# When the last three sums of weights are fetched and formed: one by one among the pairs of the first big block, with longer planned transfers

## The chip, the cores and the metric

The kernel runs on one core of a Trainium2 chip. The time is the device time of one execution in microseconds (us). Before the change the median of three runs is 609.46 us (609.19 to 609.64).

## What is computed

Chunked attention with a few memory keys (4 batches, 8 heads, 768 tokens, head width 64), and behind it a feed-forward layer on all 3072 tokens:

```
x = attention(q, k, v, mem_k, mem_v)        # 3072 x 512
h = x @ w_in                                # w_in: 512 x 2048
g = maximum(h, 0) + alpha * minimum(h, 0)
out = g @ w_out                             # w_out: 2048 x 512
```

All is float32. A product of two float32 matrices is made of three matmuls on split values: each operand is held as a high part and a low part, and low x high, high x low and high x high are added up.

## The kernel before

**Blocks.** The tokens are worked on in blocks of 384. Blocks 0 and 1 go through the layer plainly, while the rest of the attention still runs. The other six blocks form three *big blocks* of two blocks each. In a big block, `h = x @ w_in` is made by a scheme with seven products instead of eight for a 2x2 arrangement of halves: the 16 slices of `w_in` are taken in eight pairs, and for pair `i` seven products of 128x384 (named B11, B21, T2, T3, T1, T4, B22) are made by `pair(i)`, each of six matmuls (line 1174), added up on VectorE (`u`, line 1194), bent by alpha (lines 1070 and 1073) and split. Between them `pair(i)` places the second layer's matmuls (`chunk`, line 1109) of the pair before. In the first big block `pair(0)` to `pair(5)` run; the slices of the last two pairs are multiplied plainly ahead of them. Then come the second layer's remaining chunks, with two more rounds of attention between them. The second and third big block run all eight pairs.

**Weights.** A pair needs four quarters of two weight slices (`far_a[i]`, 8 pieces with their sums) and `far_b[i]` (6 pieces). They lie in DRAM and are loaded for each pair (`wa`, 1024 and 768 KB) into slots that two pairs before have given free; the second layer's weights come as `wo` (1024 KB). The original quarters are put out to DRAM while blocks 0 and 1 are worked on (`copy_far`). The *sums of weights*, which the scheme needs beside them, are made by `sum_far(i)`: GpSimd adds and subtracts quarters (`form`, lines 911 and 914), ScalarE rounds the result to the high part (a cast, line 919), GpSimd takes the low part (line 922), and SyncE puts both parts out (`put`, line 925: first to `far_b[i]`, then to `far_a[i]`). For `i` from 0 to 4 the quarters still lie in the core's memory; for the late ones, `i` = 5, 6 and 7 (`FIRST_LATE`), they are fetched back from DRAM first (`fetch`, line 904: `far_r` and the first half of `far_a`, 512 KB each). There is one set of two buffers `form`, so a fetch waits until the put before it has read its buffer out.

**Who needs the late sums.** Pair 5 of the first big block loads what `sum_far(5)` puts out. Sums 6 and 7 are first needed by pairs 6 and 7 of the second big block.

**The order of the work.** `Plan` takes the kernel's steps in program order, each with an engine, a planned cost and what it reads and writes, and sends them out by a list schedule: on each engine the ready step with the longest chain behind it goes first. A planned transfer lands `LAND` = 3.1 us behind its issue, whatever its size. What comes out is one fixed order of instructions for each engine; an engine then works strictly in that order and waits by semaphores. SyncE issues nearly all transfers, also in one order. A key such as `("gate", ...)` exists in the plan alone: it holds a step back in the order, but no semaphore is made from it. In the kernel before, all three late sums are added ahead of the pairs, gated by the last step of the plain blocks.

**Stores.** `leave` copies a finished part of the output to one of five places on its way out; three of these places are the buffers of `sum_far`.

Of the kernel before, what the change touches and what calls it, by code (L numbers as in the profile page):

```python
# [41 lines left out]
NFP = NF // 2  # L42
# [37 lines left out]
ORDER = []  # L80
# [21 lines left out]
COPY_AT = (9, 11, 13, 15, 18, 21, 24, 27)  # L102
SUM_AT = (25, 26, 28, 29, 29)
FIRST_LATE = 5
SPLIT = 0
FIRST_SLOW = 25

# [25 lines left out]
class Plan:  # L133
# [4 lines left out]
    def __init__(self):  # L138
        self.steps, self.wrote, self.read = [], {}, {}

    def add(self, engine, cost, fn, reads=(), writes=(), rest=0.0):
        n = len(self.steps)
        deps = {self.wrote[k] for k in reads if k in self.wrote}
        for k in writes:
            deps |= self.read.pop(k, set())
            if k in self.wrote:
                deps.add(self.wrote[k])
            self.wrote[k] = n
        for k in reads:
            self.read.setdefault(k, set()).add(n)  # L150
        self.steps.append((engine, cost, fn, deps - {n}, rest))

    def send(self):
        users = [[] for _ in self.steps]
        for n, step in enumerate(self.steps):
            for d in step[3]:
                users[d].append(n)
        lag = {PE: HOP, DVE: HOP, ACT: HOP, POOL: HOP, SP: LAND}
        behind = [0.0] * len(self.steps)
        for n in reversed(range(len(self.steps))):  # L160
            engine, cost, _, _, rest = self.steps[n]
            behind[n] = max(rest, cost + max((behind[m] + lag[engine] for m in users[n]), default=0.0))
        for n, more in SHIFT.items():
            behind[n] += more
        left = [len(step[3]) for step in self.steps]
        ready = [0.0] * len(self.steps)
        free = dict.fromkeys(lag, 0.0)
        able = {n for n in range(len(self.steps)) if not left[n]}
        while able:
            at = {}  # L170
            for n in able:
                engine = self.steps[n][0]
                at[engine] = min(at.get(engine, 1e9), max(ready[n], free[engine]))
            engine = min(at, key=at.get)
            n = max((n for n in able if self.steps[n][0] == engine and ready[n] <= at[engine]),
                    key=lambda n: (behind[n], -n))
            able.remove(n)
            _, cost, fn, _, _ = self.steps[n]
            free[engine] = at[engine] + cost
            fn()  # L180
            for m in users[n]:
                wait = lag[engine]
                if self.steps[m][0] == engine:
                    wait = FOLLOW if engine == DVE else 0.0
                ready[m] = max(ready[m], free[engine] + wait)
                left[m] -= 1
                if not left[m]:
                    able.add(m)
# [3 lines left out]
def body(ctx: ExitStack, tc: tile.TileContext, qvw, kw, whole, heads, w_in, w_out, alpha, out):  # L192
# [649 lines left out]

    def leave_at(late):
        n = next(ntmp)
        return MORE[n % len(MORE)] if late else PLACES[n % 2]

    def store(blk, o_ps):
        def copy(tt, at_, o):
            if blk == 1:
                o["t"] = kept[tt]  # L850
                nc.vector.tensor_tensor(out=o["t"], in0=o_ps[tt], in1=o["t"], op=ALU.add)
            else:
                o["t"] = at_[0].tile([P, DM], F32, name="o_t", tag=at_[1])
                nc.scalar.copy(out=o["t"], in_=o_ps[tt])

        def send(tt, o):
            r = blk * BT + tt * P
            nc.sync.dma_start(out=out[r:r + P, :], in_=o["t"])

        for tt in range(NTT):  # L860
            at_ = (None, None, [("tmp", tt)]) if blk == 1 else leave_at(False)
            o = {}
            place = PLACE[blk, NF - 1] + 1
            step(DVE if blk == 1 else ACT, 0.68 if blk == 1 else 0.59, partial(copy, tt, at_, o), reads=okeys(blk),
                 writes=at_[2], rest=rest(place))
            step(SP, 0.75, partial(send, tt, o), reads=at_[2])
# [25 lines left out]
    def sum_far(i, gate):  # L892
# [34 lines left out]
        whole = [[("rs", n, 0), ("rs", n, 1)] + ([("f", n, 1)] if n or late else []) for n in range(2)]  # L927
        if late:
            for n in range(2):
                step(SP, 0.75, partial(fetch, n), reads=gate + [("dr", i) if n else ("da", i, 0)], writes=whole[n] + [("f", n, 0)])  # L930

        def raw_sum(n):
            step(POOL, 1.3, partial(full, n),
# [5 lines left out]
        def form(n, to, key):  # L939
            step(ACT, 0.65, partial(high, n), reads=[("rs", n, 0), ("rs", n, 1)],  # L940
                 writes=[("f", n, 0)] + ([] if n or late else [("f", n, 1)]))
            step(POOL, 1.3, partial(low, n), reads=[("rs", n, 0), ("rs", n, 1), ("f", n, 0)], writes=[("f", n, 1)])
            step(SP, 0.7, partial(put, n, to), reads=[("f", n, 0), ("f", n, 1)], writes=[key])

        a, b = far_a[i], far_b[i]
        raw_sum(0)
# [101 lines left out]
    def big(s):  # L1048
# [7 lines left out]
        def pe(cost, fn, reads, writes):  # L1056
            step(PE, cost, fn, reads=reads, writes=writes, rest=BIG - clock[0])
            clock[0] += cost
# [101 lines left out]
        def pair(i):  # L1160
# [6 lines left out]
            def product(bank, x, weight, name):  # L1167
                xi = FORMS.index(name)

                def go():  # L1170
                    h[bank[1]] = bank_of(bank)
                    for p in range(2):
                        for k, (wk, xk) in enumerate(((0, 1), (1, 0), (0, 0))):
                            nc.tensor.matmul(  # L1174
                                out=h[bank[1]][:, :BT],
                                lhsT=weight(wk, p).bitcast(F32R),
                                rhs=xf[xi][:, xk, p],
                                start=p == 0 and k == 0, stop=p == 1 and k == 2,
                            )

                pe(1.05, go, [("wa", home["i", s, i, x])] + [("X", xi, hl, p) for hl in range(2) for p in range(2)], [bank[2]])

            def copy_out(t, bank):
                def go():
# [57 lines left out]
        def leave(which, tts, end=False):  # L1242
# [11 lines left out]
                (nc.scalar, nc.sync)[i].dma_start(out=out[r:r + P, cols], in_=x["t"][:, cols])  # L1254

            for tt in tts:
                at_, x = leave_at(True), {}
                step(ACT, 0.59, partial(copy, tt, at_, x), reads=[(downs, ups)[which][tt][2]], writes=at_[2],
                     rest=BIG - clock[0])
                if end and tt == NTT - 1:  # L1260
                    for i in range(2):
                        step((ACT, SP)[i], 0.4, partial(send_half, tt, x, i), reads=at_[2])
                else:
                    step(SP, 0.75, partial(send, tt, x), reads=at_[2])
# [26 lines left out]
        if s == 0:  # L1291
# [20 lines left out]
                plain_up(f, 1, n)  # L1312
            for f in range(12, NF):
                load(f)
            for i in range(FIRST_LATE, NFP):
                sum_far(i, [("gate", len(ORDER) - 1)])
        forms(s > 0)
        for i in pairs:
            think()
            if i in AT_PAIR[s]:  # L1320
                meet(AT_PAIR[s][i], ups)
            pair(i)
        last = s == NBIG - 1
        for f in range(2):
            take(f)
            whole(1, f)
# [156 lines left out]
```

## Time and profile before

| | us |
|---|---|
| median of three runs | 609.46 |
| the profiled execution | 609.57 |
| its span (first to last instruction) | 607.8 |
| first product of pair 0 of the first big block | 204.86 |
| last product of pair 5 | 298.00 to 299.04 |
| second layer of the first big block until the next one's first product | to 337.5 |

The profile is of one execution. A page gives busy shares, a granted TensorE clock and the share of the DMA engines; a timeline lists instructions in order, with the idle time ahead of each and, behind an arrow, what ended it. Where an instruction waits for several things, the arrow names the one that came last by the records. "PE" is TensorE, "DVE" VectorE, "ACT" ScalarE, "POOL" GpSimd, and "SPq" the queue of SyncE.

### The profile page before, as it was taken

Reading aid. Unit: us, or ns where it says so; the run is one execution under the profiler, and the core shown is the slowest. Engines: PE = TensorE matmul, PEld = TensorE weight load, DVE = VectorE, ACT = ScalarE, POOL = GpSimd, SP = SyncE. Lnnn points to the kernel's source line nnn. Section 1 sums busy time; section 2 is a strip of 40 time slices with the busy share of each in tenths; the row PEclk is TensorE's granted clock in tenths of the full one; section 3 lists DMA queues with packets and bytes.
Section 4 is the critical chain, followed back from the end, with each engine's and each line's share of the span. In section 5 each row is a group of like instructions: output and inputs, shape, how many; then the busy total and the mean of one; then the engine's idle time right before and its main releaser. Section 6 shows DMA issues by size and latency. Waiting matters only on the chain.

```text
span 607.8 us, 11965 instructions
## 1 busy us (share of the span) xinstructions
PE 578.1 (95%) x4467; PEld 510.5 (84%) x4467; DVE 458.5 (75%) x992; ACT 301.7 (50%) x780; POOL 172.8 (28%) x193
## 2 busy tenths in 40 slices
PE   6999999999999938889999999999999999999997
PEld 4889988988888827779878899999978899999785
DVE  7989999798879918778989968989748476666420
ACT  3888887656666402633655544353544333333421
POOL 5740000058989724441213700000313400000000
PEclk9999999999999977799999999999999999999999
DMA  8999960679866786797898777866796767677821
GB/s 316 392 418 415 412 267 2 221 272 335 279 241 222 254 307 213 268 326 259 320 382 308 260 262 258 297 226 212 284 362 239 248 219 272 210 272 297 312 92 52
DMA packets 43386, 164.12 MB, mean 270 GB/s; under 512 B 4928, under 2 KB 10304, under 8 KB 34624
## 3 DMA queue, kind: packets, MB, share of 16 engines
q1 hardware_dynamic: 43184, 163.23, 73.6%
q8 instruction: 35, 0.57, 0.4%
q14 instruction: 23, 0.19, 0.1%
q10 hardware_dynamic: 144, 0.13, 0.1%
HBM read 132.41 MB, written 30.93 MB: 269 GB/s over the span
## 4 chain that ended last, share of the span: by engine, by line
PE 79%; DMA 12%; DVE 5%; POOL 2%; issue 1%; SPq 0%; ACT 0%; POOLq 0%; DVEq 0%; ACTq 0%
PE b_ps L1109 25%; PE b_ps L1174 23%; PE h_ps L771 11%; PE o_ps L801 11%; DMA wo<-far_o 4%; DMA far_a<-form 3%; PE a_ps L456 2%; DMA form<-far_a 2%; PE s_ps L357 2%; DMA far_b<-form 1%; DVE xf L971 1%; DVE pt L433 1%; POOL form L914 1%; PE a_ps L616 1%; DMA early<-heads 1%; PE o_ps L603 1%
## 5 line engine op out<-in xcount | busy, mean ns | idle before, releaser
L1174 PE MATMUL b_ps<-xf,wa 128*128 128x384 f32 x924 | 179.0, 344 | 17.1 <-ACT u L1186 11.8
L1174 PEld LDWEIGHTS b_ps<-xf,wa 128*128 128x128 f32 x924 | 167.0, 193 | 25.9 <-ACT u L1186 12.3
L1194 DVE TENSOR_TENSOR u<-b_ps,u 128x384 f32<-128x384 f32 x154 | 82.9, 554 | 39.5 <-PE b_ps L1174 35.8
L433 DVE STREAM_TRANSPOSE pt<-e 32x192 f32<-32x192 f32 (+1 forms) x336 | 100.2, 302 | 10.5 <-PE a_ps L456 3.0
L1070 ACT ACTIVATE g<-u 128x384 f32<-128x384 f32 x88 | 45.9, 525 | 96.9 <-DVE u L1194 92.0
L1109 PE MATMUL b_ps<-wo,xh 128*128 128x512 f32 x276 | 86.5, 395 | 0.0
L1109 PE MATMUL b_ps<-wo,gh 128*128 128x512 f32 x276 | 86.1, 393 | 0.0
L412 POOL TENSOR_TENSOR e<-e,den 128x384 f32<-128x384 f32 x24 | 21.5, 911 | 178.1 <-ACT e L391 74.0
L771 PE MATMUL h_ps<-xh,w 128*128 128x384 f32 x256 | 65.4, 336 | 0.0
L1109 PEld LDWEIGHTS b_ps<-wo,gh 128*128 128x128 f32 x276 | 52.1, 189 | 9.9
L1109 PEld LDWEIGHTS b_ps<-wo,xh 128*128 128x128 f32 x276 | 52.0, 189 | 9.6
L1109 PE MATMUL b_ps<-wo,gl 128*128 128x512 f32 x138 | 54.5, 395 | 2.7 <-DMA wo<-far_o 2.7
L1109 PE MATMUL b_ps<-wo,xl 128*128 128x512 f32 x138 | 54.3, 394 | 0.0
L801 PE MATMUL o_ps<-w,xh 128*128 128x512 f32 x168 | 52.5, 394 | 0.0
L1073 DVE SCALAR_TENSOR_TENSOR g<-g,rise,u 128x384 f32<-128x384 f32 x44 | 30.3, 688 | 26.8 <-ACT g L1070 26.3
L771 PEld LDWEIGHTS h_ps<-xh,w 128*128 128x128 f32 x256 | 46.4, 188 | 1.0
L391 ACT ACTIVATE e<-s_ps,mx 128x64 f32<-128x64 f32 x144 | 43.1, 331 | 5.2 <-DVE mx L383 3.3
L771 PE MATMUL h_ps<-xl,w 128*128 128x384 f32 x128 | 43.8, 342 | 0.0
L985 POOL TENSOR_TENSOR plain<-plain 128x384 f32<-128x384 f32 x24 | 27.5, 1163 | 55.1 <-ACT plain L530 53.2
L801 PEld LDWEIGHTS o_ps<-w,xh 128*128 128x128 f32 x168 | 31.5, 188 | 6.1
L1109 PEld LDWEIGHTS b_ps<-wo,gl 128*128 128x128 f32 x138 | 26.1, 189 | 8.7 <-issue 2.2
L801 PE MATMUL o_ps<-w,xl 128*128 128x512 f32 x84 | 32.9, 392 | 0.0
(119 smaller groups left out, 898.6 us busy)
## 6 DMA issues: line engine op xcount, KB each, us to landing
wo<-far_o SPq DMA_DIRECT2D x46, 1024.0 KB, 7.1
wa<-far_a SPq DMA_DIRECT2D x22, 1024.0 KB, 8.7
wa<-far_b SPq DMA_DIRECT2D x22, 768.0 KB, 4.7
w_t<-w_in SPq DMA_DIRECT2D x16, 512.0 KB, 9.6
w_t<-w_out SPq DMA_DIRECT2D x16, 512.0 KB, 9.2
far_o<-w SPq DMA_DIRECT2D x16, 512.0 KB, 7.9
qk<-kw SPq DMA_DIRECT2D x24, 272.0 KB, 4.7
v_t<-qvw SPq DMA_DIRECT2D x24, 256.0 KB, 7.4
```

The costliest lines, as they stand in the source:

```text
L357: nc.tensor.matmul(out=st["s"][h2][g * CH:(g + 1) * CH, n], lhsT=qs[sets(u)][rows, c * CH:(c + 1) * CH], rhs=kbs[sets(u)][rows, t, STARTS[ ...
L391: nc.scalar.activation(out=st["e"][:, i], in_=st["s"][h2][:, n], func=AF.Exp, scale=SCALE, bias=d["mx"][:, u - us[0], n, h2:h2 + 1], accum ...
L412: nc.gpsimd.tensor_tensor(out=st["e"], in0=st["e"], in1=st["den"].broadcast_to([P, NJ * 2, KW]), op=ALU.mult)
L433: nc.vector.transpose(out=pts[u % NPT][quad * CH:(quad + 1) * CH, j, t0:t0 + n1 - n0].rearrange("p t h q -> p (t h) q"), in_=(st["e"], zer ...
L771: nc.tensor.matmul(out=h["ps"][:, :BT], lhsT=ws[f, 0][:, wk, k * P:(k + 1) * P], rhs=parts(blk, k)[1](xk), start=(k == 0 and n == 0), stop ...
L801: nc.tensor.matmul(out=o_ps[tt], lhsT=h[gk][:, tt * P:(tt + 1) * P], rhs=ws[f, 1][:, wk], start=(f == first_f and i == 0), stop=(f == last ...
L985: step(POOL, 0.95, lambda: nc.gpsimd.tensor_tensor(out=plain_at(to[0]), in0=plain_at(a[0]), in1=plain_at(b[0]), op=ALU.subtract), reads=[a ...
L1070: nc.scalar.activation(out=h[name], in_=src(), func=AF.Relu, scale=-1.0)
L1073: nc.vector.scalar_tensor_tensor(out=to() if to else h[name], in0=h[name], scalar=rise[:, f:f + 1], in1=src(), op0=ALU.mult, op1=ALU.add)
L1109: nc.tensor.matmul(out=o[which][tt], lhsT=h[gk][:, tt * P:(tt + 1) * P], rhs=w[:, wk].bitcast(F32R), start=(f == turns[which][0] and i == ...
L1174: nc.tensor.matmul(out=h[bank[1]][:, :BT], lhsT=weight(wk, p).bitcast(F32R), rhs=xf[xi][:, xk, p], start=p == 0 and k == 0, stop=p == 1 an ...
L1194: nc.vector.tensor_tensor(out=h[t], in0=h[bank[1]][:, :BT], in1=h[t if of is None else of], op=ALU.add)
```

## The change

Sum 5 is now added ahead of pair 1 and gated by pair 0's last product, sum 6 ahead of pair 4 and gated by pair 3, and sum 7 behind the last pair (pair 5) and gated by it. So the late sums begin behind the first, the fourth and the sixth pair. In the plan a late fetch now lands 8.0 us later than before (11.1 us in all), and a late put 4.0 us later. The first big block's `leave` uses three places for its stores instead of five, so that it leaves the two `form` buffers alone.

```diff
+LATE_AT = {1: 5, 4: 6}
+FETCH = 8.0
...
-    def add(self, engine, cost, fn, reads=(), writes=(), rest=0.0):
+    def add(self, engine, cost, fn, reads=(), writes=(), rest=0.0, more=0.0):
...
-                wait = lag[engine]
+                wait = lag[engine] + more
...
     def leave_at(late):
         n = next(ntmp)
-        return MORE[n % len(MORE)] if late else PLACES[n % 2]
+        return MORE[n % (2, 3, len(MORE))[late]]
...
-                step(SP, 0.75, partial(fetch, n), reads=gate + [("dr", i) if n else ("da", i, 0)], writes=whole[n] + [("f", n, 0)])
+                step(SP, 0.75, partial(fetch, n), reads=gate + [("dr", i) if n else ("da", i, 0)], writes=whole[n] + [("f", n, 0)], more=FETCH)
...
-            step(SP, 0.7, partial(put, n, to), reads=[("f", n, 0), ("f", n, 1)], writes=[key])
+            step(SP, 0.7, partial(put, n, to), reads=[("f", n, 0), ("f", n, 1)], writes=[key], more=FETCH / 2 if late else 0.0)
...
-                pe(1.05, go, [("wa", home["i", s, i, x])] + [("X", xi, hl, p) for hl in range(2) for p in range(2)], [bank[2]])
+                pe(1.05, go, [("wa", home["i", s, i, x])] + [("X", xi, hl, p) for hl in range(2) for p in range(2)],
+                   [bank[2]] + ([("pair", i)] if name == "B22" else []))
...
-                at_, x = leave_at(True), {}
+                at_, x = leave_at(1 if s == 0 else 2), {}
...
-            for i in range(FIRST_LATE, NFP):
-                sum_far(i, [("gate", len(ORDER) - 1)])
         forms(s > 0)
         for i in pairs:
+            if s == 0 and i in LATE_AT:
+                sum_far(LATE_AT[i], [("pair", i - 1)] if i else [("gate", len(ORDER) - 1)])
             think()
...
         last = s == NBIG - 1
+        if s == 0:
+            sum_far(NFP - 1, [("pair", pairs[-1])])
```

What becomes of this in the engines' orders is seen at three places. The first is ScalarE in pairs 0 and 1 of the first big block (`u`, `g`, `xh` and `gh` are the pairs' own steps, `form` a late sum's cast). Before:

```order
L1186 COPY u_2898<-b_ps_2870 128x384
L1070 ACTIVATE g_2925<-u_2898 128x384
L1085 CAST xh_209<-g_2925 128x384
L1070 ACTIVATE g_2961<-u_2949 128x384
L919 CAST form_2836<-form_2836 128x512
L1070 ACTIVATE g_2984<-u_2937 128x384
L1070 ACTIVATE g_2990<-u_2911 128x384
L919 CAST form_2900<-form_2900 128x512
L1186 COPY u_3002<-b_ps_2977 128x384
```

And with the change:

```order
L1189 COPY u_2897<-b_ps_2869 128x384
L1072 ACTIVATE g_2920<-u_2897 128x384
L1087 CAST xh_209<-g_2920 128x384
L1072 ACTIVATE g_2954<-u_2942 128x384
L1072 ACTIVATE g_2967<-u_2931 128x384
L1072 ACTIVATE g_2983<-u_2908 128x384
L1189 COPY u_2993<-b_ps_2971 128x384
```

The two casts of sum 5, which stood ahead of pair 1's copy of a product out of its bank, are gone from here. They stand now around pair 3's copy:

```order
L921 CAST form_2969<-form_2969 128x512
L1072 ACTIVATE g_3265<-u_3155 128x384
L1189 COPY u_3269<-b_ps_3246 128x384
L1087 CAST xh_215<-g_3230 128x384
L921 CAST form_2979<-form_2979 128x512
```

The second place is SyncE's queue while pairs 0 to 2 run (`wa<-far_a2` and `far_b2` are pair 2's weights, and so on; `form<-` is a fetch, `<-form` a put). Before:

```order
L904 DMA form_2900<-far_a5_232 128x1024
L295 DMA qk1_190<-qvw 128x384
L1035 DMA wa_2958<-far_b2_237 128x1536
L1035 DMA wa_2972<-far_a2_229 128x2048
L925 DMA far_b5_240<-form_2836 128x1024
L904 DMA form_3017<-far_r6_244 128x1024
L925 DMA far_a5_232<-form_2900 128x1024
L904 DMA form_3029<-far_a6_233 128x1024
L1035 DMA wa_3072<-far_b3_238 128x1536
```

And with the change:

```order
L1037 DMA wa_2951<-far_b2_237 128x1536
L1037 DMA wa_2964<-far_a2_229 128x2048
L906 DMA form_2969<-far_r5_243 128x1024
L906 DMA form_2979<-far_a5_232 128x1024
L1037 DMA wa_3054<-far_b3_238 128x1536
L1037 DMA wo_3073<-far_o3_249 128x2048
L1037 DMA wa_3098<-far_a3_230 128x2048
```

The puts of sum 5 and the fetches of sum 6 have left this stretch: the puts follow behind pair 4's loads, and the fetches of sum 6 stand on either side of pair 5's `wa<-far_a5`.

The third place is SyncE's queue around the end of pair 5 (`wo<-far_o` are the second layer's weights for the chunks that follow). Before:

```order
L1035 DMA wo_3716<-far_o2_248 128x2048
L1035 DMA wo_3733<-far_o3_249 128x2048
L1035 DMA wo_3745<-far_o1_247 128x2048
L1035 DMA wo_3789<-far_o4_250 128x2048
L1250 DMA out<-o_t_3813 128x512
```

And with the change:

```order
L927 DMA far_b6_241<-form_3373 128x1024
L927 DMA far_a6_233<-form_3392 128x1024
L1037 DMA wo_3701<-far_o2_248 128x2048
L906 DMA form_3712<-far_r7_245 128x1024
L906 DMA form_3720<-far_a7_234 128x1024
L1037 DMA wo_3775<-far_o1_247 128x2048
L1037 DMA wo_3782<-far_o3_249 128x2048
```

Sum 6's puts and sum 7's fetches stand ahead of and between the second layer's loads now. Sum 7's two puts stand 15 and 24 places behind its second fetch, among the remaining chunks' loads.

More of the change, by code (lines that the diff above doesn't have):

```diff
@@ L150, in add @@
             self.read.setdefault(k, set()).add(n)
-        self.steps.append((engine, cost, fn, deps - {n}, rest))
+        self.steps.append((engine, cost, fn, deps - {n}, rest, more))
     def send(self):
@@ L160, in send @@
         for n in reversed(range(len(self.steps))):
-            engine, cost, _, _, rest = self.steps[n]
+            engine, cost, _, _, rest, _ = self.steps[n]
             behind[n] = max(rest, cost + max((behind[m] + lag[engine] for m in users[n]), default=0.0))
@@ L177, in send @@
             able.remove(n)
-            _, cost, fn, _, _ = self.steps[n]
+            _, cost, fn, _, _, more = self.steps[n]
             free[engine] = at[engine] + cost
@@ L860, in store @@
         for tt in range(NTT):
-            at_ = (None, None, [("tmp", tt)]) if blk == 1 else leave_at(False)
+            at_ = (None, None, [("tmp", tt)]) if blk == 1 else leave_at(0)
             o = {}
```

## The prediction, made before the changed kernel ran

> **What bounds the kernel now.** I read the windows of busy time first, one for each stage around the change.
>
> ```profile
> core 0: us, PE busy (x) PEld busy (x) DVE busy (x) ACT busy (x) POOL busy (x), PEclk, DMA share, GB/s
> 204.90:217.40 12.50, 12.50 (x66) 11.32 (x66) 9.54 (x21) 3.08 (x7) 5.08 (x5) 1.00 0.69 224
> 217.40:229.20 11.80, 0.02 (x1) 0.00 (x0) 1.55 (x2) 2.47 (x6) 4.49 (x5) 0.64 0.72 274
> 229.20:245.50 16.30, 13.02 (x77) 11.50 (x77) 11.46 (x27) 4.26 (x10) 7.38 (x8) 0.81 0.72 250
> 245.50:271.60 26.10, 24.46 (x111) 22.19 (x111) 20.43 (x45) 11.88 (x41) 12.69 (x12) 0.88 0.79 288
> 271.60:299.00 27.40, 27.40 (x248) 25.32 (x249) 24.32 (x64) 13.07 (x45) 3.96 (x4) 0.94 0.78 276
> 299.00:337.50 38.50, 37.28 (x394) 29.95 (x393) 34.42 (x93) 22.58 (x83) 9.81 (x10) 1.00 0.94 342
> ```
>
> TensorE is the bound everywhere but in one place: from 217.4 to 229.2 us it does nothing, and behind that its granted clock is 0.81 and 0.88. This is the stage of the six pairs. TensorE's timeline gives its edges and waits:
>
> ```profile
> 204.86 11.17 PE L1174 MATMUL b_ps<-xf,wa 128*128 128x384 f32 x60 [0.27 <-DVE plain L1073]
> ...
> 229.24 2.29 PE L1174 MATMUL b_ps<-xf,wa 128*128 128x384 f32 x6 [11.82 <-ACT u L1186]
> ...
> 245.53 4.21 PE L1174 MATMUL b_ps<-xf,wa 128*128 128x384 f32 x12 [3.28 <-ACT plain L530]
> ...
> 271.60 4.96 PE L1174 MATMUL b_ps<-xf,wa 128*128 128x384 f32 x18 [1.60 <-DVE u L1194]
> ...
> 298.00 1.21 PE L1174 MATMUL b_ps<-xf,wa 128*128 128x384 f32 x6
> ```
>
> The three waits inside the stage make 11.82 + 3.28 + 1.60 = 16.7 us. What stands behind them is read from ScalarE's timeline:
>
> ```profile
> 212.21 0.53 ACT L1070 ACTIVATE g<-u 128x384 f32<-128x384 f32 x1 [0.87 <-DVE u L1194]
> 226.57 0.62 ACT L919 CAST form<-form 128x512 fp32r<-128x512 f32 x1 [13.84 <-DMA wa<-far_b]
> ...
> 228.71 0.47 ACT L1186 COPY u<-b_ps 128x384 f32<-128x384 f32 x1
> ...
> 244.07 0.62 ACT L919 CAST form<-form 128x512 fp32r<-128x512 f32 x1 [5.42 <-POOL form L914]
> ...
> 264.83 0.62 ACT L919 CAST form<-form 128x512 fp32r<-128x512 f32 x1 [4.62 <-POOL form L914]
> ```
>
> ScalarE stands for 13.84, 5.42 and 4.62 us ahead of a late sum's cast, and the copy that frees TensorE's bank is queued behind that cast. The arrow of the first wait names a load of `wa`, which a cast of `form` has no need of; I take it for a neighbour in time, since GpSimd and SyncE show the true chain:
>
> ```profile
> 224.48 1.26 POOL L911 TENSOR_TENSOR form<-form 128x512 f32<-128x512 f32 x1 [10.63 <-DMA form<-far_a]
> ...
> 211.38 0.59 SPq L925 DMA_DIRECT2D far_a<-form  x1
> 220.06 0.32 SPq L904 DMA_DIRECT2D form<-far_a  x1
> ```
>
> GpSimd waits 10.63 us for the fetch; that was issued at 220.06 only, 8.7 us behind the put that had to read the same buffer out.
>
> **What the change removes.** By the orders above, pair 1's copy has no cast ahead of it any more. I build the stage again without its waits, from steady rows of the third big block and this stage's attention steps:
>
> ```profile
> 496.43 4.33 PE L1174 MATMUL b_ps<-xf,wa 128*128 128x384 f32 x24
> 500.60 0.39 PE L1109 MATMUL b_ps<-wo,gl 128*128 128x512 f32 x1
> ...
> 501.30 0.39 PE L1109 MATMUL b_ps<-wo,gl 128*128 128x512 f32 x1
> ...
> 512.06 0.39 PE L1109 MATMUL b_ps<-wo,xl 128*128 128x512 f32 x1
> ...
> 284.86 1.20 PE L357 MATMUL s_ps<-qk 64*32 64x64 f32 x96
> 285.99 1.54 PE L456 MATMUL a_ps<-pt,v_t 128*64 128x96 f32 x32
> 287.46 3.41 PE L1174 MATMUL b_ps<-xf,wa 128*128 128x384 f32 x18
> ```
>
> 24 matmuls (four products) take 500.60 - 496.43 = 4.17 us, so a product 1.04; a chunk of three takes 0.70; a whole pair (seven products, six chunks) 512.06 - 500.60 = 11.46. Scores take 1.13 us and attention outputs 1.47. The stage has pair 0 with seven products alone (7.3), five full pairs (57.3), one round of scores and two of outputs (4.1): **68.7 us**. It took 298.00 + 1.04 - 204.86 = 94.2. So **25.5 us** are lost: 16.7 by waits, 0.3 of rounding and gaps, and 8.5 by the clock. The clock's part is seen in the same rows: the six matmuls at 229.24 took 2.29 us where six take 1.04, the twelve at 245.53 took 4.21 where twelve take 2.08; and the windows agree, 16.3 x 0.19 + 26.1 x 0.12 + 27.4 x 0.06 = 7.9 us.
>
> The page "TensorE: Matmul & The Clock Gate" of the Trainium skill (The HAM clock gate) says that the array runs at half clock after an idle window of about 3.4 us and again at full clock after about 3.4 us of work. By that rule only the 11.82 us wait costs clock for certain, 1.7 us, and the whole gain would be some 18.7 us in place of 25.5. The rows disagree: behind waits of 3.28 and 1.60 us the matmuls are slow as well, so the sum goes by the rows.
>
> **What it adds: casts, fetches, puts.** Nothing new is computed; each late sum keeps its two fetches, two casts, GpSimd steps and two puts. The question is whether the moved ones wait again. Sum 5's fetches now follow pair 2's loads, which wait for pair 0's end, 204.86 + 7.3 = 212.2. Queued behind them on SyncE are pair 3's loads, and these wait for pair 1's last uses of their slots, about 10 us later, so no load is held. The casts stand around pair 3's first copy; pair 3 starts at 212.2 + 11.5 + 11.5 + 1.5 = 236.7.
>
> ```profile
> wa<-far_a SPq DMA_DIRECT2D x6, 1024.0 KB, 9.5
> ...
> form<-far_a SPq DMA_DIRECT2D x3, 512.0 KB, 4.3
> ```
>
> A fetch lands 4.3 us behind its issue; even at 9.5, what a load of twice the size took in this stretch, it is there by 224, and four GpSimd steps of 1.3 us at most (the L911 row) end by 230. That leaves 6 us before the cast. Sum 6 is fetched when pair 3 ends, 248.2, and cast in pair 5, which starts at 248.2 + 11.5 + 2.6 = 262.3; sum 7 is cast among the remaining chunks. I cost them at nothing, the pairs' matmuls cover them; if that cover were gone, each would cost what the second and third cast do now (a rival below). Pair 5 needs sum 5's puts: cast at 237 to 239 and with a GpSimd step behind, they go out at about 241, and pair 5's load, which waits for their landing, can go at 248.2 anyway.
>
> **What is late next: VectorE.** From 214.8 us, when it had worked off what was left from the plain blocks, to the stage's end:
>
> ```profile
> 214.80:299.05 84.25, 67.54 (x451) 61.08 (x450) 57.81 (x135) 31.73 (x100) 28.51 (x27) 0.86 0.77 275
> ```
>
> VectorE is busy for 57.81 us there, and TensorE's own need is 68.7 - 9.9 = 58.8: 98%, with both waiting for each other in a fixed order. From 271.6 to 299 VectorE ran at 24.32 / 27.40 = 0.89 with TensorE never idle. At 0.89 the stretch takes 65.0 us (6.2 more than TensorE's need), at 1 it takes nothing more. Since nobody waited for VectorE at 0.89, that row is no ceiling; I take 0.93, nearer to it than to 1: 62.2, so **3.4 us** come back.
>
> **The transfers.** Six of 512 KB (puts and fetches of sums 6 and 7), 3.1 MB, move from the pairs into the stage of remaining chunks, whose engines are 0.94 busy at 342 GB/s; at that rate they are 9.2 us of transfers, against 0.06 x 38.5 = 2.3 us of room: at worst 6.9 us. Not all is due, since loads for the next big block stand at that stage's end. SyncE also waits there: sum 7's fetches wait for sum 6's puts to land, and `wo<-far_o1` is queued behind them.
>
> ```profile
> far_a<-form SPq DMA_DIRECT2D x5, 512.0 KB, 5.0
> ...
> wo<-far_o SPq DMA_DIRECT2D x46, 1024.0 KB, 7.1
> ...
> 308.63 0.47 PE L1109 MATMUL b_ps<-wo,gl 128*128 128x512 f32 x1 [1.22 <-DMA wo<-far_o]
> ```
>
> That stage had one wait for such a load, 1.22 us. The load's slot is free when pair 5 ends; its issue comes about 5 us (a put's landing) behind sum 6's puts, and its first use 12 chunks, 8.3 us, behind the pair, plus 1.1 for the scores that now stand between. Bounds are -1.2 (that wait goes too) and +6.9; I take **+1.0**, nearest to the row. Five places to three for stores and the plan's longer landing only order things: 0, as ScalarE is busy 22.58 of 38.5 us there.
>
> **The sum.** 609.57 (this execution; 0.1 above the median of 609.46) - 25.5 + 3.4 + 1.0 = **588.5 us**, -3.5%. With both ends: 609.6 - 25.5 - 1.2 = 582.9, and 609.6 - 25.5 + 6.2 + 6.9 = 597.2.
>
> **Rivals.**
>
> *VectorE becomes the bound.* If its steps and TensorE's wait for each other as in 245.5 to 271.6 (20.43 of 26.10, 0.78), 57.8 us become 74, so 15 of the 25.5 us come back: 609.6 - 25.5 + 15.3 = 599.4. For it speaks the 98%; against it the 0.89 of a stretch without any wait, and that the 0.78 holds ScalarE's waits that go.
>
> *Transfers bound the remaining chunks.* All 6.9 us at worst, and half clock behind the waits (+2.5 as at 245.53 and after): 609.6 - 25.5 + 3.4 + 9.4 = 596.9. For it speaks 0.94; against it that loads with later dates can give way.
>
> *The casts wait again in their new places*, as the second and third did (3.28 + 1.60, and the clock after them 2.1 + 1.8), some 9 us, with VectorE's 3.4 and 1.0: 597.3. Against it speaks the 6 us of room.
>
> *The change does not take the first wait away*, because the load that the arrow names was the cause: then 11.8 us and 4 of clock stay, 609.6 - 9.7 + 3.4 + 1 = 604.3. Against it: a cast needs no `wa`, and in the new order those loads stand earlier anyway.
>
> *Slower.* SyncE holds the second layer's loads behind sum 6's puts. If these puts wait for GpSimd, and that for attention's steps ahead of it, each us counts from the point where `wo<-far_o1` is issued later than pair 5's end + 9.4 - 7.1 (a load's landing). To eat up 25.5 us the puts would have to be 20 us and more behind pair 5; their casts stand in its first half, so this would need several late landings in a row: over 612.
>
> **Chances.** Forecast (583 to 593) 0.55; VectorE 0.18; transfers 0.10; casts again 0.07; first wait stays 0.04; slower 0.05; nothing either way 0.01. The range of 583 to 599 holds the first, the third, the fourth and half of VectorE's: 0.81. A measurement tells 0.2% from no change here. Faster by more 0.93, within 0.02, slower 0.05.
>
> **What would show it.** Right: pair 1 follows pair 0 without a wait; no cast of `form` has over 2 us of idle time ahead of it in the pairs; granted clock 0.97 and more from 217 to 275; pair 5 ends near 277 instead of 299; VectorE over 0.9 busy. Wrong: a wait of TensorE for `wo` above 3 us behind pair 5, many waits for `u` of VectorE, or SyncE standing at `far_b6`'s put while slots for `wo` are free.

## The result, and the profile after

The changed kernel takes **586.74 us** (median of 4 runs, 585.58 to 587.69) beside 609.33 us (606.64 to 609.64) of the kernel before: ratio **0.9638**, 95% interval 0.9604 to 0.9672. Its profiled execution took 586.14 us with a span of 584.4, so 23.4 us less than the one before in both. One of the four executions of experiment 2 below took 632.85 us at a granted clock of 0.85 and is left out of its ratio. The lines have moved by two or three: L1174, L1109, L919 and L904 of before are L1176, L1111, L921 and L906 now.

The windows of busy time after the change: the six pairs (204.90 to 275.00), the same without what VectorE had left from the plain blocks, the remaining chunks, the second big block's first layer, its first few chunks, and the rest.

```profile
core 0: us, PE busy (x) PEld busy (x) DVE busy (x) ACT busy (x) POOL busy (x), PEclk, DMA share, GB/s
204.90:275.00 70.10, 70.01 (x502) 64.08 (x502) 65.15 (x158) 33.36 (x103) 25.63 (x24) 1.00 0.89 326
214.80:275.00 60.20, 60.20 (x450) 54.87 (x449) 55.63 (x136) 29.09 (x94) 22.44 (x21) 1.00 0.88 324
275.00:313.00 38.00, 37.20 (x393) 30.05 (x393) 35.78 (x91) 24.27 (x87) 18.78 (x18) 1.00 1.02 401
313.00:412.50 99.50, 99.50 (x744) 91.21 (x743) 85.36 (x201) 44.46 (x127) 18.51 (x19) 1.00 0.70 252
412.50:422.70 10.20, 8.82 (x40) 7.05 (x39) 4.42 (x9) 4.94 (x10) 0.00 (x0) 1.00 0.94 371
422.70:584.40 161.70, 157.09 (x814) 138.36 (x814) 86.69 (x165) 53.81 (x106) 13.67 (x12) 1.00 0.64 228
```

TensorE is busy for all of the 60.20 us from 214.8 on, at a granted clock of 1.00; the window with 0.02 us of work and the clocks of 0.81, 0.88 and 0.94 have no counterpart any more. TensorE's timeline after the change gives the edges, and every wait of TensorE from 204 us to the end that the view marks:

```profile
204.98 11.19 PE L1176 MATMUL b_ps<-xf,wa 128*128 128x384 f32 x60 [0.26 <-DVE plain L1075]
216.01 0.39 PE L1111 MATMUL b_ps<-wo,xl 128*128 128x512 f32 x1
...
275.06 1.24 PE L359 MATMUL s_ps<-qk 64*32 64x64 f32 x96
...
285.04 0.47 PE L1111 MATMUL b_ps<-wo,gl 128*128 128x512 f32 x1 [0.36 <-DVE mx L385]
...
304.62 0.50 PE L1111 MATMUL b_ps<-wo,xl 128*128 128x512 f32 x1 [0.44 <-DVE xl L1091]
...
312.95 1.22 PE L1176 MATMUL b_ps<-xf,wa 128*128 128x384 f32 x6
...
422.71 0.47 PE L1111 MATMUL b_ps<-wo,gl 128*128 128x512 f32 x1 [1.39 <-DMA wo<-far_o]
...
551.67 0.47 PE L1111 MATMUL b_ps<-wo,gl 128*128 128x512 f32 x1 [0.64 <-DMA wo<-far_o]
```

From these two views the 23.4 us are put in their places. The points are the first product of pair 0, the end of the pair stage (the first instruction with all 42 products and 30 chunks done: a chunk at 299.04 before, scores at 275.06 after), the first product of the second big block (337.37 and 312.95), and the span's end (607.8 and 584.4).

| stretch | before | after | difference |
|---|---|---|---|
| up to pair 0 | 204.86 | 204.98 | +0.1 |
| six pairs and their chunks | 94.2 | 70.1 | -24.1 |
| remaining chunks | 38.3 | 37.9 | -0.4 |
| second big block to the end | 270.4 | 271.4 | +1.0 |

So the pairs gave all of it. ScalarE's timeline after the change shows the casts of the late sums in their new places, of which the first four are in the pairs:

```profile
237.12 0.62 ACT L921 CAST form<-form 128x512 fp32r<-128x512 f32 x1
...
239.70 0.62 ACT L921 CAST form<-form 128x512 fp32r<-128x512 f32 x1
...
266.00 0.61 ACT L921 CAST form<-form 128x512 fp32r<-128x512 f32 x1
...
267.30 0.62 ACT L921 CAST form<-form 128x512 fp32r<-128x512 f32 x1
...
292.83 0.62 ACT L921 CAST form<-form 128x512 fp32r<-128x512 f32 x1 [3.33 <-POOL form L916]
...
300.57 0.62 ACT L921 CAST form<-form 128x512 fp32r<-128x512 f32 x1
```

None of the four in the pairs has idle time ahead of it. The one at 292.83 waits 3.33 us for GpSimd, and no wait of TensorE is marked behind it until 304.62. GpSimd's timeline after the change shows how early sum 5 is ready:

```profile
221.99 2.55 POOL L913 TENSOR_TENSOR form<-form 128x512 f32<-128x512 f32 x2 [13.90 <-DMA form<-far_r]
224.50 3.88 POOL L916 TENSOR_TENSOR form<-form 128x256 f32<-128x256 f32 x4
```

It is formed at 228.4, and the cast stands at 237.1: 8.7 us of room.

### The profile page after: what moved, and what is told of

Read it like the earlier page. It is cut to its first block, busy times and chain, and to the rows that moved or that the text cites. A ratio compares the mean times of both kernels' runs of the same rounds, so it can differ in the third digit from the quotient of the medians.

```text
span 584.4 us, 11961 instructions
## 1 busy us (share of the span) xinstructions
PE 572.0 (98%) x4467; PEld 505.0 (86%) x4467; DVE 458.2 (78%) x992; ACT 302.0 (52%) x780; POOL 173.0 (30%) x193
## 4 chain that ended last, share of the span: by engine, by line
PE 85%; DVE 6%; DMA 4%; POOL 2%; issue 2%; ACT 0%; SPq 0%; POOLq 0%; DVEq 0%; ACTq 0%
PE b_ps L1176 28%; PE b_ps L1111 26%; PE h_ps L773 12%; PE o_ps L803 11%; DMA wo<-far_o 3%; PE a_ps L458 2%; DVE pt L435 2%; PE s_ps L359 2%; DVE xf L973 1%; PE a_ps L618 1%; DMA early<-heads 1%; PE o_ps L605 1%; PE b_ps L1147 1%; PE s_ps L334 1%; POOL early L224 1%
## 5 line engine op out<-in xcount | busy, mean ns | idle before, releaser
L1176 PE MATMUL b_ps<-xf,wa 128*128 128x384 f32 x924 | 172.9, 336 | 0.3 <-DVE plain L1075 0.3
L1176 PEld LDWEIGHTS b_ps<-xf,wa 128*128 128x128 f32 x924 | 161.8, 188 | 8.1 <-DVE u L1197 1.1
L1111 PE MATMUL b_ps<-wo,xh 128*128 128x512 f32 x276 | 86.0, 393 | 0.0
L1111 PE MATMUL b_ps<-wo,gh 128*128 128x512 f32 x276 | 85.7, 392 | 0.0
L1111 PEld LDWEIGHTS b_ps<-wo,gh 128*128 128x128 f32 x276 | 51.8, 188 | 9.9
L1111 PEld LDWEIGHTS b_ps<-wo,xh 128*128 128x128 f32 x276 | 51.8, 188 | 9.6
L1111 PE MATMUL b_ps<-wo,gl 128*128 128x512 f32 x138 | 54.2, 392 | 2.4 <-DMA wo<-far_o 2.0
L1111 PE MATMUL b_ps<-wo,xl 128*128 128x512 f32 x138 | 54.4, 394 | 0.4 <-DVE xl L1091 0.4
L1111 PEld LDWEIGHTS b_ps<-wo,gl 128*128 128x128 f32 x138 | 25.9, 188 | 8.3 <-issue 2.8
```

The source lines that it names most:

```text
L1111: nc.tensor.matmul(out=o[which][tt], lhsT=h[gk][:, tt * P:(tt + 1) * P], rhs=w[:, wk].bitcast(F32R), start=(f == turns[which][0] and i == ...
L1176: nc.tensor.matmul(out=h[bank[1]][:, :BT], lhsT=weight(wk, p).bitcast(F32R), rhs=xf[xi][:, xk, p], start=p == 0 and k == 0, stop=p == 1 an ...
```

## The experiments

Each ratio is to the kernel before, on the same chip. "The change" means the changed kernel, of which a second set of six runs, beside the last three experiments, gave 587.60 us (585.41 to 589.27; 0.9636, 0.9604 to 0.9668):

> The change itself once more, beside the next three on one chip. 585.5 to 588.5; TensorE without a wait from 205.3 us to the end of pair 5, 0.3 to 0.8 us in the remaining chunks, 1 to 1.5 us at the second big block's loads.

It repeats the result to 0.9 us, so differences of about 1 us between experiments are not told apart. Its profile has no wait in the pairs and 0.80 us behind them, as expected, but 2.55 us at the second big block's first `wo`, where 1 to 1.5 were expected. A profile is of one execution; where that one lies far from its kernel's median, the text says so.

### 1. Is the cast the cause, or the load that the arrow named?

In the kernel before, the late casts go to GpSimd; no other step changes, and the plan makes its order anew.

```diff
-            nc.scalar.copy(out=t[n][:, 0].bitcast(F32R), in_=r[n])
+            (nc.gpsimd.tensor_copy if late else nc.scalar.copy)(out=t[n][:, 0].bitcast(F32R), in_=r[n])
...
-            step(ACT, 0.65, partial(high, n), ...
+            step(*((POOL, 1.3) if late else (ACT, 0.65)), partial(high, n), ...
```

> The kernel before, with the late sums' two casts on GpSimd instead of ScalarE, so that ScalarE never stands for a late sum; SyncE's order in the pairs stays as before (fetch of sum 5 ahead of pair 2's loads, puts and fetches ahead of pair 3's). Theory A (the cast in ScalarE's queue held pair 1's copy): the 11.8 us wait of TensorE at pair 1 goes wholly; pair 2's loads still leave at about 221.5 and land at 231, due 226.7, so a wait of some 4 us comes there, and pair 3's loads behind puts and fetches cost about 8 to 10 more; time 598 to 604. Rival (the load of wa that the arrow names was the cause): the wait at pair 1 stays at 10 to 12 us and the time at 607 to 610.

Measured: 604.62 us (10 runs, 600.24 to 607.78), 0.9911 (0.9877 to 0.9945), just above the 598 to 604 that I expected; the profiled execution took 601.85. TensorE's timeline of this kernel:

```profile
218.24 1.28 PE L1174 MATMUL b_ps<-xf,wa 128*128 128x384 f32 x6 [0.53 <-DMA wa<-far_b]
...
228.80 3.38 PE L1174 MATMUL b_ps<-xf,wa 128*128 128x384 f32 x18 [0.95 <-DMA wa<-far_a]
...
249.82 6.03 PE L1174 MATMUL b_ps<-xf,wa 128*128 128x384 f32 x18 [9.65 <-DMA wa<-far_a]
...
265.61 3.36 PE L1174 MATMUL b_ps<-xf,wa 128*128 128x384 f32 x18 [1.42 <-DMA wa<-far_a]
```

The wait of 11.82 us at pair 1 is gone, and 0.53 us is all that a load of `wa` holds there. So the cast was the cause of TensorE's wait, and not the load. But only some 5 us come off the time, since a wait of 9.65 us stands at pair 3 instead. SyncE's timeline of this kernel shows why:

```profile
230.84 0.32 SPq L925 DMA_DIRECT2D far_b<-form  x1
233.43 0.32 SPq L904 DMA_DIRECT2D form<-far_r  x1
233.85 0.37 SPq L925 DMA_DIRECT2D far_a<-form  x1
238.96 0.32 SPq L904 DMA_DIRECT2D form<-far_a  x1
239.33 0.42 SPq L1035 DMA_DIRECT2D wa<-far_b  x1
239.85 0.38 SPq L1035 DMA_DIRECT2D wo<-far_o  x1
240.33 0.40 SPq L1035 DMA_DIRECT2D wa<-far_a  x1
```

Pair 3's loads go out in one run behind the puts of sum 5 and the fetches of sum 6. The queue stood 9.6 us at the first put, which waits for GpSimd, and 2.2 and 4.7 us at the two fetches, which wait for the put before them to read its buffer out. Two causes, then: ScalarE's order and SyncE's. Taking away the first uncovers the second.

### 2 and 3. The places alone, and the planned landing alone

The change has both; each was run without the other. Experiment 2 is the change with one number changed (it keeps the three places for stores):

```diff
-FETCH = 8.0
+FETCH = 0.0
```

Experiment 3 is the kernel before with the longer landing alone:

```diff
-            step(SP, 0.75, partial(fetch, n), ...)
+            step(SP, 0.75, partial(fetch, n), ..., more=FETCH)
...
-            step(SP, 0.7, partial(put, n, to), ...)
+            step(SP, 0.7, partial(put, n, to), ..., more=FETCH / 2 if late else 0.0)
```

> The change with the longer planned landing taken out (8.0 and 4.0 us to 0). The sums keep their late gates; the plan sets sum 5's casts ahead of pair 2's copy instead of around pair 3's. Theory A (what counts is that fetches stand behind loads and casts come late): fetches leave at 213 to 216, forms are ready at 226 to 229, pair 2's copy is due at 228, so 0 to 3 us of waits come back: 587 to 591. Rival (the planned landing does the work): casts are planned too early in each sum and two or three waits of 3 to 5 us with half clock come back: 595 to 602.

> The kernel before with only the longer planned landing of late fetches and puts; all late sums still added ahead of the pairs and five places for stores. The casts move behind pair 1's copy, but the first fetch of sum 5 still stands ahead of pair 1's loads and the second ahead of pair 2's, each waiting for a put to land. Theory A: the wait at pair 1 goes, SyncE still stands until 220 and pair 2 waits 4 to 5 us for its load, with half clock behind it: 592 to 597. Rival (casts alone held TensorE): 586 to 588. Rival (the gates alone do it): 606 to 610.

Measured, 2: 0.9779 (0.9717 to 0.9841), some 596 us (595.33, 595.51 and, profiled, 599.05). I had expected 587 to 591; the rival had it. Measured, 3: 596.41 us, 0.9775 (0.9718 to 0.9832), as expected. ScalarE's timeline of the second kernel has the casts' waits back, and TensorE's has one wait behind each:

```profile
227.85 0.62 ACT L921 CAST form<-form 128x512 fp32r<-128x512 f32 x1 [6.21 <-POOL form L916]
...
268.45 0.62 ACT L921 CAST form<-form 128x512 fp32r<-128x512 f32 x1 [5.83 <-POOL form L916]
```

```profile
231.18 4.21 PE L1176 MATMUL b_ps<-xf,wa 128*128 128x384 f32 x12 [2.93 <-ACT plain L532]
...
272.50 2.83 PE L458 MATMUL a_ps<-pt,v_t 128*64 128x96 f32 x32 [4.68 <-DVE u L1197]
```

With a landing of 3.1 us in the plan, the cast of sum 5 stands earlier in ScalarE's order, before GpSimd is done; it runs at 227.85 (237.12 in the change) after a wait of 6.21 us. In the third kernel the casts wait up to 3.63 us without a wait of TensorE for them, and a load is late, as in experiment 1. TensorE's largest wait there:

```profile
271.49 6.13 PE L1176 MATMUL b_ps<-xf,wa 128*128 128x384 f32 x18 [4.81 <-DMA wa<-far_a]
```

So the two parts mend different things: the landing moves casts behind the forms, the places move fetches and puts behind the pairs' loads. Alone, each gains about 13.5 us (0.022 x 609); together 22, so the two gains overlap.

### 4. Five places for the stores

```diff
-                at_, x = leave_at(1 if s == 0 else 2), {}
+                at_, x = leave_at(2), {}
```

> The change with five places for the first big block's stores again, so that a late sum's buffers and the output's parts take turns. I costed the three places at 0: 586 to 588. Rival: stores and sum 7 wait for each other's buffers, SyncE and the second layer's loads behind: 589 to 594.

Measured: 593.30 us, 0.9726 (0.9675 to 0.9776), so 5.7 to 6.6 us slower than the two sets of the change; I had expected 586 to 588, and the rival had it. The pairs are without waits here too; the loss is behind them. ScalarE's and TensorE's timelines of this kernel:

```profile
301.67 0.59 ACT L1249 COPY o_t<-b_ps 128x512 f32<-128x512 f32 x1 [1.61 <-DMA far_b<-form]
303.22 0.59 ACT L1249 COPY o_t<-b_ps 128x512 f32<-128x512 f32 x1 [0.54 <-DMA far_a<-form]
```

```profile
286.84 0.50 PE L1111 MATMUL b_ps<-wo,gl 128*128 128x512 f32 x1 [2.22 <-DVE gl L1091]
...
303.86 1.54 PE L458 MATMUL a_ps<-pt,v_t 128*64 128x96 f32 x32 [0.95 <-ACT o_t L1249]
...
327.86 1.83 PE L1176 MATMUL b_ps<-xf,wa 128*128 128x384 f32 x9 [1.26 <-DVE xf L973]
331.12 6.51 PE L1176 MATMUL b_ps<-xf,wa 128*128 128x384 f32 x36 [1.43 <-DVE u L1197]
```

Copies of finished output wait for sum 7's puts, whose buffers they take. That is 0.95 us of TensorE directly; the rest stands in waits for VectorE, in an order that the plan made otherwise, with sum 7's GpSimd steps 5.1 us earlier (281.37 against 286.50). That three places are worth some 6 us is shown; how they come about is shown for those 0.95 us only.

### 5. How near is VectorE to the bound?

In the first big block, two low parts of each pair are made twice on VectorE, with the same result: 12 more steps of 0.55 us.

```diff
-                (nc.gpsimd if slow else nc.vector).tensor_tensor(out=h["gl"], ...
+                for _ in range(2 if s == 0 and name != "g" else 1):
+                    (nc.gpsimd if slow else nc.vector).tensor_tensor(out=h["gl"], ...
```

> The change, with each pair's two low parts on VectorE in the first big block done twice (12 steps of 0.55 us more, 6 us, the second one the same as the first; order and plan unchanged). In the pairs VectorE was busy 55.6 of 60.2 us with TensorE never waiting. Theory B (VectorE had 4 to 5 us of real room there): what exceeds the room comes out as waits of TensorE, 1 to 3 us, time 588 to 590. Rival (VectorE was nearly the bound already, any step shows): waits of 5 us and more, time 592 and more. Rival (VectorE is far from the path): no change, 586 to 587.5.

Measured: 592.34 us, 0.9712 (0.9672 to 0.9752), where I had expected 588 to 590; the rival of 592 and more had it. 6.6 us of VectorE work cost 4.7 to 5.6 us. TensorE waits for VectorE five times in the pairs now; the largest of these waits:

```profile
273.87 1.74 PE L1177 MATMUL b_ps<-xf,wa 128*128 128x384 f32 x6 [1.78 <-DVE u L1198]
```

The five waits make 3.85 us, and over the 4 us behind the longest the granted clock is 0.58, which is 1.7 us more. So VectorE is the next bound in the pairs. Its room in the change is some 2 to 3 us by these waits (6.6 - 3.85), an estimate from one execution.

### 6. How near are the transfers?

The puts of sums 6 and 7 are issued twice with the same data: 2.1 MB more.

```diff
-            nc.sync.dma_start(out=to.rearrange("p (l m) -> p l m", l=2), in_=t[n].bitcast(F32))
+            for _ in range(2 if i > FIRST_LATE else 1):
+                nc.sync.dma_start(out=to.rearrange("p (l m) -> p l m", l=2), in_=t[n].bitcast(F32))
```

> The change, with the puts of sums 6 and 7 issued twice (four transfers of 512 KB more, 2.1 MB, all behind pair 5's start). Theory C (in the remaining chunks the transfers run at 401 GB/s but most have time): sum 7's fetches wait some 3 us longer for the doubled puts, the load of the second layer's weights behind them is late, one wait of 1 to 4 us; 587.5 to 591. Rival (transfers are the bound there): all of 2.1 MB / 401 GB/s = 5.2 us and half clock come out, 592 and more. Rival (room for everything): 586 to 587.5.

Measured: 600.34 us (593.30 to 602.11, the last one profiled), 0.9825 (0.9758 to 0.9891): 13 us lost, more than the 587.5 to 591 that I expected and nearest to the rival of 592 and more. SyncE's and TensorE's timelines of this kernel:

```profile
268.81 6.47 SPq L928 DMA_DIRECT2D far_b<-form  x2
275.37 4.39 SPq L928 DMA_DIRECT2D far_a<-form  x2
```

```profile
291.69 0.76 PE L1112 MATMUL b_ps<-wo,gl 128*128 128x512 f32 x1 [6.71 <-DMA wo<-far_o]
...
339.95 4.90 PE L1177 MATMUL b_ps<-xf,wa 128*128 128x384 f32 x18 [3.42 <-DMA wa<-far_a]
```

2.1 MB at the 401 GB/s of this stretch are 5.2 us; the loss is more than twice that, because the queue stands 6.47 and 4.39 us at the doubled puts, with loads of `wo` behind them (a single put is 0.33 us there in the change), and 10.15 and 8.27 us at sum 7's. By SyncE's waits, each second put stands until the first has landed (25.9 us over all four), so the doubling holds the queue beside adding bytes. The experiment doesn't part the two, and how much rate the remaining chunks have to spare stays open; that a held queue is dear without any bytes added is seen in experiment 8.

### 7 and 8. Other places, a longer landing

Experiment 7 is the change with sum 6 right behind sum 5 (the first edit), experiment 8 the change with a planned landing of 14 us (the second).

```diff
-LATE_AT = {1: 5, 4: 6}
+LATE_AT = {1: 5, 2: 6}
...
-FETCH = 8.0
+FETCH = 14.0
```

> The change with sum 6 gated by pair 1 instead of pair 3; its fetches then stand ahead of pair 5's loads and its puts ahead of pair 0's loads for the next big block. Theory A (order against due dates is all that counts): pair 5's loads leave behind a fetch that waits for a put of 5 to 9 us, 1 to 4 us of waits; 587 to 592. Rival (any order with late casts does): 585.5 to 587.5.

> The change with 14 us of planned landing more in place of 8 (7 for puts); up to pair 5 SyncE's order is the same, behind it the load of the second layer's weights stands ahead of sum 7's fetches. Theory A: the pairs stay without waits, the remaining chunks lose their 0.8 us of waits at most: 585.5 to 588. Rival (steps pushed back later in the plan cost as in the five places): 589 to 593.

Measured, 7: 591.33 us, 0.9690 (0.9651 to 0.9729), in the expected range of 587 to 592, but not for the expected reason: in the profiled execution, the fastest with 588.51 us, the two waits that are new in the pairs stand behind VectorE (1.73 and 0.87 us), and no load is late in the pairs. What made the others some 3 us slower no trace shows. Measured, 8: 593.17 us, 0.9729 (0.9696 to 0.9762); I had expected 585.5 to 588, and the rival said 589 to 593. SyncE's and TensorE's timelines of the eighth kernel:

```profile
274.02 0.38 SPq L927 DMA_DIRECT2D far_b<-form  x1
282.92 0.32 SPq L906 DMA_DIRECT2D form<-far_r  x1
283.33 0.38 SPq L927 DMA_DIRECT2D far_a<-form  x1
288.29 0.32 SPq L906 DMA_DIRECT2D form<-far_a  x1
```

```profile
308.25 2.83 PE L458 MATMUL a_ps<-pt,v_t 128*64 128x96 f32 x32 [4.61 <-DMA v_t<-qvw]
```

A landing that is planned too long brings sum 6's puts 5.5 and 13.0 us later (they are at 268.55 and 270.30 in the change). Each fetch of sum 7 follows such a put into the same buffer, so that SyncE stands for 8.9 us and again for 5.0, and loads behind go late: the one of `v_t` that TensorE waits 4.61 us for leaves at 297.00 (290.27 in the change). With `FETCH` at 0, 8 and 14 a fetch is planned to land 3.1, 11.1 and 17.1 us behind its issue; the change's fetches took 6.6 us, by the median. Of these three the middle one is best, though it is 4.5 us above what the fetches took; no value between was run.

### 9 to 11. Sums 6 and 7 in the second big block

They are first needed there. In the first of these kernels, sum 5 stays behind the first pair and sums 6 and 7 go behind the first and third pair of the second big block (its pairs 0 and 2); in the next, only sum 7 moves, behind pair 1 there, with `{(0, 1): 5, (0, 4): 6, (1, 2): 7}`; the third is the first of them with five places for stores, the last edit here.

```diff
-LATE_AT = {1: 5, 4: 6}
+LATE_AT = {(0, 1): 5, (1, 1): 6, (1, 3): 7}
...
-            if s == 0 and i in LATE_AT:
-                sum_far(LATE_AT[i], [("pair", i - 1)] if i else [("gate", len(ORDER) - 1)])
+            if (s, i) in LATE_AT:
+                sum_far(LATE_AT[s, i], [("pair", i - 1)])
...
-        if s == 0:
-            sum_far(NFP - 1, [("pair", pairs[-1])])
...
-                at_, x = leave_at(1 if s == 0 else 2), {}
+                at_, x = leave_at(2), {}
```

> The change with sums 6 and 7 moved on into the second big block (behind its pairs 0 and 2), whose pairs 6 and 7 are the first to need them. Six transfers of 512 KB leave the remaining chunks of the first big block (401 GB/s, 1.02 busy) for a stage at 252 GB/s and 0.70. Theory C (transfers and SyncE's order in the remaining chunks are what is tight now): the waits there stay under 1 us and the transfers' share falls to 0.94, nothing new in the second block: 584.5 to 587. Rival (the second block's loads have no more room than the first's): waits of 2 to 5 us for wa in its pairs 4 to 7: 588 to 592.

> The change with sum 7 alone moved into the second big block, behind its pair 1. Theory C: as the one before, between it and the change: 585 to 587.5. Rival: 588 and more.

> The run with both sums in the second big block, and with five places for the first block's stores. Theory (the five places cost 6 us because sum 7 and the output's parts took turns in two buffers): with no late sum left in that stage five places cost nothing, the time is that of three places within 1 us. Rival (five places are dear by themselves): 4 to 7 us more than with three.

Measured: 586.47 us (0.9625, 0.9596 to 0.9655), 586.35 us (0.9621, 0.9592 to 0.9651) and 589.41 us (0.9662, 0.9629 to 0.9695). Windows of the first, over the remaining chunks and the second block's first layer:

```profile
275.00:313.00 38.00, 36.84 (x392) 29.59 (x391) 34.00 (x93) 22.17 (x82) 9.68 (x10) 1.00 0.93 342
313.00:412.50 99.50, 99.07 (x742) 90.94 (x741) 87.58 (x199) 46.59 (x132) 38.03 (x35) 1.00 0.80 293
```

The transfers leave the full stretch (0.93 in place of 1.02) for one that had room (0.80 in place of 0.70), and the time is that of the change within the intervals: what the change gave those transfers was cover enough. Five places cost some 3 us here, half of what they cost with the late sums in that stage; I had expected at most 1, the rival 4 to 7. In the profiled executions none of it lies in the stage of the stores: from the end of the pairs to the second big block's first product the third kernel (590.77 us in that execution) takes 38.0 us and the first 38.2. Behind that, TensorE's timeline of the third kernel has waits for `wo` of 2.72 us at 425.00 (and a granted clock of 0.57 over the next 4 us) and 1.36 at 556.30, where the first has 0.94 at 422.66 and none marked later; why stores' places should bring them is open, and the change itself had 2.55 us at the same `wo` in its second set. None of these kernels beats the change by more than can be measured.

## Why the prediction came out

Predicted were 588.5 us (583 to 599) and measured 586.7, so the forecast held. By its steps:

**What the change removes** was right, and its cause too: pair 1 follows pair 0 without a wait, and experiment 1 shows that the cast, not the load of the arrow, had held it. The stage became 24.1 us shorter, where the sum had 25.5 - 3.4 = 22.1.

**The clock's part** (8.5 us) was right in going by the rows, and too large: of the 24.1 us, 16.7 are the three waits, which leaves 7.4 for the clock and the gaps, where the sum had 8.5 and 0.3. The difference is the 1.4 us by which the rebuilt stage was too short (see VectorE). The Trainium skill, "TensorE: Matmul & The Clock Gate" (The HAM clock gate), has half clock come after an idle window of about 3.4 us; by the estimate that the prediction drew from it, the stage could not have become more than 18.7 us shorter. Experiment 2 speaks against that rule once more: behind a wait of 2.93 us twelve matmuls took 4.21 us at a granted clock of 0.50, where the prediction's steady row gives 2.08.

**VectorE** was mis-sized: +3.4 predicted, and no wait for VectorE is marked in the pairs. The stage is 1.4 us longer than rebuilt (70.1 against 68.7), but not by such waits. Its share came out as 55.63 / 60.20 = 0.92, almost the 0.93 that I took, but that was no ceiling: TensorE's work filled the stretch itself. The rebuilt stage was a little short: the ten products at 204.98 took 11.03 us up to the next instruction, 1.10 each, where I had 1.04; that is 0.6 of the 1.4. That VectorE stands close behind was right (experiment 5).

**The casts** cost nothing, as predicted; the room ahead of sum 5's cast is 8.7 us, not 6. Their rival is real, though: it is what experiment 2 shows, where the casts wait again and the time is some 9 us longer than the change's.

**Transfers:** +1.0 predicted, -0.4 measured. The stretch carried 401 GB/s, where I had reckoned with the 342 of before as its rate, and the wait for `wo` of 1.22 us went away, as in my lower bound (-1.2). How near the upper bound was stays open: 2.1 MB more cost 13 us (experiment 6), but its doubled puts held the queue as well.

**Five places to three, and the longer landing: "only order things: 0".** This step was wrong twice over. Taken out of the change, the landing costs some 9 us (experiment 2) and the three places some 6 (experiment 4). The sum did not suffer, because I costed casts and transfers at the places where the orders of the whole change had put them, and that order has both edits in it. As a price for each edit alone the zeros were wrong; my argument, that ScalarE had time left in the remaining chunks, does not bear on a copy that waits for a buffer.

**Not foreseen:** +1.0 us from the second big block on. Of it 0.43 and 0.15 are longer waits for `wo` (1.39 against 0.96, 0.64 against 0.49). The second set of the change has 2.55 us at the first of these places, with a granted clock of 0.57 over the 4 us behind it, so that wait differs from one execution to the next, and the 1.0 is no firm effect of the change.

**Rivals.** That the first wait stays was ruled out by experiment 1 as well as by the result. The slower case, SyncE held at sum 6's puts with loads of `wo` behind them, did not come about, but experiments 6 and 8 show it in kernels where the puts hold the queue, at 6 to 13 us.

So the 588.5 came near through terms that were off by 2.0, 1.4 and 1.0 us, the first two in one direction and the last in the other. The 2.0 is itself what is left of 3.4 too much for VectorE and 1.4 too little for the rebuilt stage. That errors of both directions met in this way was luck.

## What to carry to other kernels

On an engine that works in order, a step that waits for a transfer costs what is queued behind it: look for the idle time ahead of cheap steps (here a cast of 0.62 us with 13.84 us before it), and see what stands next in line. A plan that takes transfers to land earlier than they do puts such steps too early (experiment 2); one that takes them to land far too late moves the wait to the queue that issues them (experiment 8). Here a planned 11.1 us, above the measured 6.6, was the best of three. And where several edits make one new order, price the order as a whole; what each is worth is seen only by taking it out again.

## What the runs showed of the hardware

**A short wait can slow the clock, and one as long may not.** These are all waits of TensorE over 1.2 us from pair 0 on, in all kernels here, with the mean granted clock over the 4 us behind each.

| waits, us | where | clock behind |
|---|---|---|
| 1.22 to 1.59 (twelve) | nine kernels | 1.00 |
| 1.60, 1.78, 2.00 | before, experiments 5 and 6 | 0.57, 0.58, 0.57 |
| 1.73, 1.89, 1.92, 2.22 | experiments 7, 10, 4 and 4 | 1.00 |
| 2.55 to 11.82 (eleven) | eight kernels | 0.50 to 0.68 |

Between 1.6 and 2.2 us both happen, so the length of the wait alone does not decide it; what does, no run here shows. At full clock, eighteen matmuls of products take 3.31 us (the change, 320.39). Behind waits of 0.95 and 1.42 us they took 3.38 and 3.36 (experiment 1), behind 4.81 and 9.65 us 6.13 and 6.03 (experiments 3 and 1).

**VectorE's steps stretch beside GpSimd.** In the change, 79 of the subtractions of line 1091 had no GpSimd step beside them and took 0.56 us at most. Of the 17 that had one, twelve took 0.60 to 1.65 us and five 0.56 or less. VectorE's timeline of experiment 4 shows both kinds, where GpSimd was adding from 281.37 to 288.2:

```profile
283.10 1.54 DVE L1091 TENSOR_TENSOR xl<-gs,xh 128x384 fp32r<-128x384 f32 x1
...
285.24 0.55 DVE L1091 TENSOR_TENSOR xl<-gs,xh 128x384 fp32r<-128x384 f32 x1
285.70 1.08 DVE L1091 TENSOR_TENSOR gl<-gs,gh 128x384 fp32r<-128x384 f32 x1
```

The Trainium skill, "SBUF — State Buffer" (SBUF: two separate sides), has the two engines share one pair of ports, of which one is shut out for a whole instruction of the other; this holds for a VectorE step with two inputs in that memory beside a GpSimd step that reads it. The rows agree with that as far as they go, some steps long and others not; no run here tests it. It may be a part of why TensorE waits for VectorE in experiment 7; this was not tested.

**The transfers of one core** carried 401 GB/s over 38 us in the remaining chunks, with no wait of TensorE for a load.
